# Attention before a soft mixture of experts: block maxima one step earlier, the last batch's slot sums in column halves, A scaled on VectorE, the denominator applied in the relu

## The chip, the cores and the metric

The kernel runs on one core of a Trainium2 chip. The time is device time of one execution in microseconds. The engines of the core are TensorE (PE in the profile, its weight loads PEld), VectorE (DVE), ScalarE (ACT), GpSimd (POOL) and SyncE (SP), which here issues nearly all DMA transfers.

## What is computed

Three layers follow one another, all in float32. The first is a local and block-summary attention over 4 batches, 8 heads, 768 positions and 64 columns per head. A query sees the 31 keys around it, and 24 summaries: the maximum over each block of 32 keys, with the mean of the block's values.

```python
k_sum = k.reshape(B, H, nb, block, D).max(axis=3)
v_sum = v.reshape(B, H, nb, block, D).mean(axis=3)
scores_l = scale * np.matmul(q, k.transpose(0, 1, 3, 2))
scores_s = scale * np.einsum('bhsd,bhnd->bhsn', q, k_sum) + np.log(block)
a = softmax(np.concatenate([np.where(mask_l, scores_l, -1e9), scores_s], axis=-1))
x = np.matmul(a, np.concatenate([v, v_sum], axis=2))     # 3072 tokens x 512
```

The second layer is a soft mixture of 8 experts with 4 slots each. Its slots are sums over all tokens, so nothing of its experts can start before the last token of the attention is through:

```python
logits = x @ phi                                          # 3072 x 32
d = exp(logits - logits.max(0)); d /= d.sum(0) + 1e-9     # over the tokens
slot_input = d.T @ x                                      # 32 x 512
slot_out[e] = np.maximum(slot_input[e] @ w1[e], 0) @ w2[e]
x = softmax(logits, axis=1) @ slot_out
```

The third layer routes each token to the nearest of 8 expert embeddings and applies that expert with a gate.

## The kernel before

**The attention loop.** The unit is a pair of heads (16 pairs: 4 per batch), and each pair has two steps `u` of 384 positions. The even step is u = 2m, the odd one 2m + 1. The loop `for u in range(NU + 11)` with NU = 32 writes out the order of the work by hand: each engine runs its instructions in the order in which the loop emits them. Step u emits the scores `s_pe(u)` (TensorE, tile `s`), the masked maxima `s_max(u)` (VectorE, L316), the subtraction `s_sub(u)` (GpSimd, L329), then for the step two before the product with the values `v_pe(u - 2)` (TensorE, tile `po`, a single PSUM bank) and its division `v_norm` (VectorE, tile `X`), then block sums of the values (`vs`, `vs2`, spread by GpSimd at L267 in even steps), transposes `x_pe` and logits `x_log` of earlier pairs, then the transposes `p_pe(u - 1)` of the probabilities (tile `pt`, copied to `pts` by ScalarE) and at the end the exponentials `s_exp(u)` (ScalarE).

The scores of a pair read keys and block maxima from one tile `kT`. The maxima are made by `t_sum(n)` on VectorE in four instructions (L276, L277, L284, L285): two reductions over 16 keys into `hm`, and two that combine halves into the places in `kT`. In the kernel before, the odd step 2m + 1 ends with `t_sum(m + 1)`, and the next step begins with the scores that read it.

**The slot sums.** `moe_a(b)` takes the running maximum of a batch's logits (`nm_run`, L420) and the exponentials, `moe_b` transposes, `moe_c` multiplies with `X` (TensorE, tile `pa`, L481) and its `moe_c_ev` rescales `A_run` by `al` and adds (L495). `moe_d` makes the combine weights `ce_all` (L507 to L518) in three consecutive steps. For the last batch (b = 3) this is written out at step U_END = 37: `A_run` is scaled by a matmul with the diagonal `dal` (L474), the slots' maxima and denominators go through `si_max`, `si_bc` and `si_den`, the denominator enters the weights `wsl`, and `siT_done` makes `siT` by four matmuls (tile `psi`, L569). Single `keep_warm` matmuls (L589) stand between. The experts' first product `ph` (L756) reads `siT`.

**The loads.** SyncE issues all loads in order: for pair m + 3 at the odd step 2m + 1 its `kT` (484 KB, three buffers), `qT` (384 KB), and two `vw` (390 KB each), and weight tiles of 1024 KB by the list W_STEPS, one every second step up to step 24. A load waits at the head of the queue until its buffer is free. The 32 weight tiles lie in buffers that the attention leaves: `big2` holds `kT`, `qT` and the masked scores, the tile number W_X takes the buffer of an `X`. The first sixteen feed `ph`, the others the product `pO` (L832).

Of the kernel before, what the change touches and what calls it, by code (L numbers as in the profile page):

```python
# [134 lines left out]
def tile_kernel(ctx, tc, qT, kTd, vwd, phi, w1, w2, emb, tau, u1, u2, consts, consts2, out):  # L135
# [11 lines left out]
    siT = cp.tile([P, 4, NSLOT], F32, name="siT")  # L147
    c0r = cp.tile([P, 1], BF16, name="c0r")
# [55 lines left out]
    with ExitStack() as es:  # L204
# [222 lines left out]
        def moe_a2(b):  # L427
            nm, prev = nm_run[:, b : b + 1], nm_run[:, b - 1 : b]
            if b:
# [11 lines left out]
                if b == B - 1:  # L441
                    dal = p3.tile([96, 96], F32, name="dal", bufs=1)
                    nc.vector.tensor_scalar_mul(dal, ident[:96, :96], al)
                    st_["dal"] = dal
# [11 lines left out]
        def moe_b_ev(b):  # L456
            L = sp.tile([P, 2, 2, 96], F32, tag="L", name=f"L{b}")
            pn = st_.pop(("pn", b))
            if b < B - 1:
                nc.vector.tensor_copy(L, pn)  # L460
            else:
                nc.vector.tensor_copy(L[:, 1], pn[:, 1])
                nc.scalar.copy(L[:, 0], pn[:, 0])
            st_["L", b] = L

        def moe_c(b, part=None):

            last = b == B - 1
            if part in (None, 0):
                st_["pa", b] = ps_tr.tile([P, 512], F32, tag="tr", name=f"pa{b}")[0:96, :]  # L470
            pa = st_["pa", b]
            if part == 0:
                for g in range(3):
                    nc.tensor.matmul(  # L474
                        pa[32 * g : 32 * g + 32, :], st_["dal"][:, 32 * g : 32 * g + 32], A_run, start=True, stop=False
                    )
                return
            L, X = st_["L", b], st_["X", b]
            for j in range(2) if part is None else (part - 1,):
                for g in range(3):  # L480
# [4 lines left out]
                        start=j == 0 and not last,  # L485
# [3 lines left out]
        def moe_c_ev(b):  # L489
            pa = st_.pop(("pa", b))  # L490
            if b == B - 1:
                nc.vector.tensor_copy(A_run[:, 0:256], pa[:, 0:256])
                nc.scalar.copy(A_run[:, 256:512], pa[:, 256:512])
            elif b:
# [27 lines left out]
        def si_max():  # L522

            pm = ps_s.tile([P, 512], F32, tag="s", name="pm")
            st_["pm"] = pm
            nc.tensor.transpose(pm[0:1, 0:96], nm_run[:, B - 1 : B], ident[:96, :96])

        def si_max_ev():
            gm = sp.tile([1, NSLOT], F32, tag="gm", name="gm")
            gm3 = sp.tile([1, 3, NSLOT], F32, tag="gm3", name="gm3")  # L530
            nc.vector.tensor_reduce(
                gm, st_["pm"][0:1, 0:96].rearrange("p (g s) -> p s g", g=3), axis=AX.X, op=ALU.min
            )
            nc.vector.tensor_copy(gm3, gm.unsqueeze(1).to_broadcast([1, 3, NSLOT]))
            st_["gm3"] = gm3

        def si_bc():
            nc.tensor.matmul(
                st_["pm"][:96, 96:97], st_["gm3"].rearrange("p g s -> p (g s)"), ones[0:1, 0:1],
                start=True, stop=True,  # L540
            )

        def si_bc_ev():
            gmc = sp.tile([96, 1], F32, tag="gmc", name="gmc")
            fw = sp.tile([96, 2], F32, tag="fw", name="fw")
            nc.vector.tensor_copy(gmc, st_["pm"][:96, 96:97])
            nc.scalar.activation(fw[:, 0:1], nm_run[:, B - 1 : B], AF.Exp, bias=gmc, scale=-1.0)
            nc.vector.tensor_tensor(out=fw[:, 1:2], in0=fw[:, 0:1], in1=sm_run[:, B - 1 : B], op=ALU.mult)
            st_["fw"] = fw

        def si_den():
            pd = ps_s.tile([P, 512], F32, tag="s", name="pd")
            nc.tensor.matmul(pd[:96, 0:1], con[:96, C_SEL : C_SEL + 96], st_["fw"][:, 1:2], start=True, stop=True)
            st_["pd"] = pd

        def si_den_ev():
            rd = sp.tile([96, 1], F32, tag="rd", name="rd")
            wsl = sp.tile([96, NSLOT], F32, tag="wsl", name="wsl")
            nc.vector.tensor_scalar_add(rd, st_["pd"][:96, 0:1], 1e-9)
            nc.vector.reciprocal(rd, rd)  # L560
            nc.vector.tensor_tensor(out=rd, in0=rd, in1=st_["fw"][:, 0:1], op=ALU.mult)
            nc.vector.tensor_scalar_mul(wsl, con[:96, C_SEL : C_SEL + NSLOT], rd)
            st_["wsl"] = wsl

        def siT_done():

            psi = ps_s.tile([P, 512], F32, tag="s", name="psi")
            for c in range(4):
                nc.tensor.matmul(  # L569
                    psi[:, c * NSLOT : (c + 1) * NSLOT], A_run[:, c * P : (c + 1) * P], st_["wsl"],  # L570
                    start=True, stop=True,
                )
            nc.vector.tensor_copy(siT.rearrange("p c s -> p (c s)"), psi[:, 0 : 4 * NSLOT])

        def warm_up():
# [3 lines left out]
            for _ in range(5):  # L579
# [33 lines left out]
        for u in range(NU + 11):  # L613
# [7 lines left out]
            if inr(u - 2):  # L621
# [3 lines left out]
                v_norm(u - 2)  # L625
            if u == 1:
# [13 lines left out]
            if (n := at(u, 4, 2, NPAIR)) is not None:  # L640
                x_pe(n, 1)
                x_ev(n, 1)
# [748 lines left out]
```

## Time and profile before

| | |
|---|---|
| Median of three runs | 275.32 us (273.88 to 280.05) |
| The profiled execution | 275.28 us, of which the profile's span is 273.4 us |
| TensorE busy | 237.8 us, 87% of the span |
| VectorE busy | 152.0 us, 56% |
| ScalarE busy | 127.1 us, 46% |
| GpSimd busy | 90.9 us, 33% |
| Moved by DMA | 72.53 MB, mean 265 GB/s |

The span runs from the first to the last instruction of the program. An engine is counted as busy while one of its instructions runs; waiting is not counted. The attention fills the first 150 us or so, then come the slot sums, the experts of the second layer (to about 202 us), and the third layer. The chain of waits follows the work that ended last back to the start: at each step to what released it. "Idle before" is the time in which an engine had nothing to do, with the instruction that ended it.

### The profile page before, as it was taken

The page shows a single profiled execution, that of the slowest core. Times are in us where ns is not written, and L with a number is a line of the kernel's source. Part 1 is how long each engine was busy: PE and PEld are TensorE (multiplying, and loading weights), DVE is VectorE, ACT ScalarE, POOL GpSimd, SP SyncE. Part 2 cuts the span into 40 slices and gives each one's busy share as a digit, 9 for nine tenths or more (in the row PEclk, how much of TensorE's full clock was granted, in tenths as well). Part 3 has the DMA queues.
Part 4 walks back from the last instruction along what each step waited for, and adds up shares of the span by engine and source line. Part 5 has one row for each costly group of instructions (what it writes and reads, how often), then busy time and mean ns, then how long its engine had stood idle before and what let it go on. Part 6 is the DMA issues. An engine that isn't in the chain of part 4 may idle for free.

```text
span 273.4 us, 7963 instructions
## 1 busy us (share of the span) xinstructions
PE 237.8 (87%) x3070; PEld 156.3 (57%) x3070; DVE 152.0 (56%) x698; ACT 127.1 (46%) x290; POOL 90.9 (33%) x131
## 2 busy tenths in 40 slices
PE   4798988998898878988898899999899998869980
PEld 1477676776766666667675443333375662637760
DVE  2567766767667677587764531133211676645840
ACT  1366456555546556355644311142323677733650
POOL 0456546654475536545642000000101560010000
PEclk9999999999999999999999999999999979977997
DMA  6999989999869997774399999999397000002993
GB/s 212 400 399 386 386 308 331 333 332 334 299 242 339 314 343 256 295 255 136 96 339 316 363 382 380 387 386 380 102 330 283 1 0 1 2 29 95 340 382 113
DMA packets 33658, 72.53 MB, mean 265 GB/s; under 512 B 2712, under 2 KB 4504, under 8 KB 33616
## 3 DMA queue, kind: packets, MB, share of 16 engines
q1 hardware_dynamic: 33552, 71.77, 73.8%
q8 instruction: 26, 0.43, 0.7%
q0 software_dynamic: 64, 0.20, 0.2%
q14 instruction: 16, 0.13, 0.2%
HBM read 65.67 MB, written 6.29 MB: 263 GB/s over the span
## 4 chain that ended last, share of the span: by engine, by line
PE 62%; DVE 23%; DMA 4%; issue 3%; ACT 3%; POOL 1%; SPq 1%; DVEq 0%; ACTq 0%
PE s L301 10%; DVE fix L316 7%; PE po L356 5%; PE ph L756 5%; PE pt L343 5%; PE pO L832 5%; DVE hm L277 4%; PE pht L1049 4%; PE lp L407 3%; DVE X L373 3%; DMA w2e<-in_moe_w_dram 3%; PE pa L481 3%; PE py L1292 2%; PE pd L261 2%; PE py L1294 2%
## 5 line engine op out<-in xcount | busy, mean ns | idle before, releaser
L329 POOL TENSOR_TENSOR fix<-fix,nb 128x360 f32<-128x360 f32 x64 | 49.2, 789 | 62.5 <-DVE nb L316 62.4
L316 DVE CUSTOM_DVE_ANT_0 fix<-s,con 128x120 f32<-128x120 f32 x192 | 41.7, 279 | 35.5 <-PE s L301 35.5
L344 ACT COPY pts<-pt 120x384 f32<-120x384 f32 x64 | 27.6, 482 | 15.1 <-PE pt L343 15.0
L335 ACT ACTIVATE fix<-fix 128x360 f32<-128x360 f32 x64 | 29.2, 510 | 8.3 <-POOL fix L329 8.3
L356 PE MATMUL po<-vw,pts 120*64 120x65 f32 x768 | 29.9, 226 | 1.4 <-POOL vw L267 0.5
L356 PEld LDWEIGHTS po<-vw,pts 120*64 120x64 f32 x768 | 25.3, 137 | 6.9 <-ACT pts L344 3.1
L343 PE MATMUL pt<-con,fix 128*120 128x128 f32 x192 | 27.1, 276 | 0.7 <-ACT fix L335 0.7
L267 POOL COPY vw<-vw 24x780 f32<-24x780 f32 x31 | 25.8, 833 | 3.4 <-issue 1.5
L301 PE MATMUL s<-fix,fix 64*64 64x120 f32 x480 | 19.0, 272 | 8.3 <-DVE fix L284 7.9
L343 PEld LDWEIGHTS pt<-con,fix 128*120 128x120 f32 x192 | 21.1, 138 | 7.3 <-issue 6.2
L301 PEld LDWEIGHTS s<-fix,fix 64*64 64x64 f32 x480 | 14.0, 132 | 12.7 <-DVE fix L284 10.0
L373 DVE TENSOR_TENSOR X<-po,den 128x384 f32<-128x384 f32 x32 | 17.9, 558 | 1.1
L399 ACT COPY xT<-tx 128x384 f32<-128x384 f32 x32 | 15.3, 480 | 6.5 <-PE tx L389 5.7
L1062 DVE CUSTOM_DVE_ANT_0 hlo<-pht,scr 128x1024 fp32r<-128x1024 f32 x11 | 13.3, 1213 | 8.6 <-PE pht L1049 8.6
L389 PE MATMUL tx<-con,X 128*128 128x128 f32 x96 | 16.7, 283 | 0.7 <-DVE X L373 0.7
L1049 PE MATMUL pht<-cT,gs 128*128 128x512 f32 x48 | 16.0, 457 | 0.7 <-ACT hhi L1073 0.5
L1073 ACT ACTIVATE hhi<-pht,scr 128x1024 fp32r<-128x1024 f32 x13 | 14.5, 1116 | 3.7 <-PE pht L1049 3.5
L257 ACT COPY vw<-pd 128x130 f32<-128x130 f32 x16 | 4.3, 268 | 25.6 <-PE pd L261 25.6
L301 PE MATMUL s<-fix 64*64 64x120 f32 x288 | 11.4, 272 | 5.5 <-DVE fix L284 4.8
L316 DVE DVE_READ_ACCUMULATOR2_ANT nb<- 128x1 f32 x192 | 16.0, 83 | 0.2
L832 PE MATMUL pO<-w,hx 128*32 128x512 f32 (+1 forms) x152 | 15.4, 509 | 0.0
L277 DVE TENSOR_REDUCE hm<-fix 128x48 f32<-128x768 f32 x16 | 15.1, 945 | 0.4 <-DMA fix<-in_kT_dram 0.4
(233 smaller groups left out, 371.8 us busy)
## 6 DMA issues: line engine op xcount, KB each, us to landing
w<-in_moe_w_dram SPq DMA_DIRECT2D x30, 1024.0 KB, 9.4
vw<-in_vw_dram SPq DMA_DIRECT2D x32, 390.0 KB, 6.9
fix<-in_kT_dram SPq DMA_DIRECT2D x15, 484.0 KB, 5.3
out_dram<-Y SPq DMA_DIRECT2D x24, 256.0 KB, 2.7
fix<-in_qT_dram SPq DMA_DIRECT2D x15, 384.0 KB, 5.8
w1e<-in_moe_w_dram SPq DMA_DIRECT2D x4, 512.0 KB, 4.5
w2e<-in_moe_w_dram SPq DMA_DIRECT2D x4, 512.0 KB, 9.1
wx<-in_moe_w_dram SPq DMA_DIRECT2D x1, 1024.0 KB, 8.3
```

What stands on the lines that cost most here:

```text
L267: (nc.scalar.copy if n == 0 and par else nc.gpsimd.tensor_copy)(st_["vw", n][row0 : row0 + NB, par].rearrange("p (s x) -> p s x", s=6), vo ...
L277: nc.vector.tensor_reduce(hm[:, 1:49].rearrange("p (c b) -> p c b", b=8), kT[:, 32 + NB :].rearrange("p (c x) -> p c x", x=152)[:, :, 0:12 ...
L301: nc.tensor.matmul(sp[j][64 * i : 64 * i + 64, c, :], qns[n % 3][64 * j : 64 * j + 64, 64 * t : 64 * t + 64], kTs[n % 3][64 * j : 64 * j + ...
L316: nc.vector.tensor_tensor_reduce(out=sms[u % 2][:, j, c, :], in0=sp[:, c, :], in1=con[:, m0 : m0 + KW], scale=-0.125, scalar=3.0e38, op0=A ...
L329: nc.gpsimd.tensor_tensor(out=sm, in0=sm, in1=st_["nb", u][:, j].unsqueeze(2).to_broadcast([P, 3, KW]), op=ALU.subtract)
L335: nc.scalar.activation(sm, sm, AF.Exp, scale=-1.0)
L343: nc.tensor.transpose(pt[:, c, :], sms[u % 2][:, j, c, :], ident)
L344: nc.scalar.copy(pts[:, j], pt)
L356: nc.tensor.matmul(po[64 * i : 64 * i + 64, c, j, :], pts[:, j, c, 64 * i : 64 * i + 64], vw[:KW, i, x0 : x0 + 65], start=True, stop=True,)
L373: nc.vector.tensor_tensor(out=X[:, 3 * h : 3 * h + 3, 2 * hp * D : (2 * hp + 2) * D].rearrange("p c (j d) -> p c j d", j=2), in0=po[:, :, ...
L832: nc.tensor.matmul(po[c][32 * g : 32 * g + 32, 0 : cs.stop - cs.start], hTs[r][:, fc, 32 * g : 32 * g + 32], w[:, g, cs], start=(r, fc) in ...
L1049: nc.tensor.matmul(ph[:, c * 512 : c * 512 + 512], G[:, k * P : (k + 1) * P], cTt(1024 * j + 512 * c, 512), start=True, stop=True,)
```

## The change

It does five things. `t_sum(m + 1)` is emitted at the end of the even step 2m, no longer at the end of the odd step 2m + 1. In the last batch's slot sums `A_run` is scaled and added to on VectorE, as in the other batches, and not by a matmul with `dal`; the sums are made in two column halves with a `psi` of their own. The denominator no longer enters `wsl`: its reciprocal goes into `rdm`, which replaces the constant scale of the relu. `moe_c` of the third batch is split over steps 33 and 34, `moe_d` comes two steps later for every batch, the last `p_pe` comes ahead of the other work of step 32, and the loop is two steps longer. The warm-up has two matmuls, before five, and three weight tiles change their buffers or steps.

```diff
-W_X, W_BIG2, W_BIG3 = 17, (13, 14, 16, 18), (20, 21)
+W_X, W_BIG2, W_BIG3 = 19, (13, 14, 16, 17), (20, 21)
-W_STEPS = (*range(4, 26, 2), 27, 29, 30, 30, 31, 32, 32, 33, 33)
+W_STEPS = (*range(4, 26, 2), 27, 29, 30, 30, 31, 32, 33, 33, 34)
...
+        def moe_last(b):
...
+            nc.vector.tensor_reduce(nm, lp, axis=AX.X, op=ALU.max, negate=True)
+            nc.vector.tensor_tensor(out=nm, in0=nm, in1=prev, op=ALU.min)
+            keep_warm(4)
+            pm = ps_s.tile([P, 512], F32, tag="s", name="pm")
+            nc.tensor.transpose(pm[0:1, 0:96], nm, ident[:96, :96])
+            nc.scalar.activation(LT[:, 1, :], lp, AF.Exp, bias=nm, scale=1.0, accum_out=smb)
+            nc.scalar.activation(al, prev, AF.Exp, bias=nm, scale=-1.0)
+            nc.vector.tensor_reduce(gm, pm[0:1, 0:96].rearrange("p (g s) -> p s g", g=3), axis=AX.X, op=ALU.min)
+            keep_warm(1)
...
+            for j in range(2):
+                nc.tensor.transpose(pn[1][:, 96 * j : 96 * j + 96], LT[:, 1, j * P : j * P + P], ident[:96, :96])
+            nc.scalar.copy(L[:, 1].rearrange("p j x -> p (j x)"), pn[1])
+            pg = ps_s.tile([P, 512], F32, tag="s", name="pg")
+            for g in range(3):
+                nc.tensor.matmul(pg[32 * g : 32 * g + 32, 0:1], gm, ones[0:1, 0:1], start=True, stop=True)
+            keep_warm(1)
+            nc.vector.tensor_copy(gmc, pg[:96, 0:1])
+            nc.scalar.activation(fw[:, 0:1], nm, AF.Exp, bias=gmc, scale=-1.0)
+            nc.vector.scalar_tensor_tensor(
+                out=smb, in0=sm_run[:, b - 1 : b], scalar=al, in1=smb, op0=ALU.mult, op1=ALU.add
+            )
+            nc.vector.tensor_copy(LT[:, 0, :], lp)
+            nc.vector.tensor_tensor(out=fw[:, 1:2], in0=fw[:, 0:1], in1=smb, op=ALU.mult)
+            nc.vector.tensor_scalar_mul(wsl, sel[:, 0:NSLOT], fw[:, 0:1])
+            psi = []
+            for i in range(2):
+                pa = ps_s.tile([P, 512], F32, tag="s", name=f"pl{i}")[0:96, 0:256]
+                for j in range(2):
+                    for g in range(3):
+                        nc.tensor.matmul(
+                            pa[32 * g : 32 * g + 32, :],
+                            L[:, 1, j, 32 * g : 32 * g + 32],
+                            X[:, 2 * g + j, half[i]],
+                            start=j == 0,
+                            stop=j == 1,
+                        )
+                nc.vector.scalar_tensor_tensor(
+                    out=A_run[:, half[i]], in0=A_run[:, half[i]], scalar=al, in1=pa, op0=ALU.mult, op1=ALU.add
+                )
+                if i == 0:
...
+                    nc.tensor.matmul(pd[:, 0:1], sel, fw[:, 1:2], start=True, stop=True)
+                    for j in range(2):
+                        nc.tensor.transpose(
+                            pn[0][:, 96 * j : 96 * j + 96], LT[:, 0, j * P : j * P + P], ident[:96, :96]
+                        )
+                    nc.scalar.copy(L[:, 0].rearrange("p j x -> p (j x)"), pn[0])
+            for i in range(2):
+                psi.append(ps_s.tile([P, 512], F32, tag="s", name=f"psi{i}"))
+                for c in range(2):
+                    x0 = (2 * i + c) * P
+                    nc.tensor.matmul(
+                        psi[i][:, c * NSLOT : (c + 1) * NSLOT], A_run[:, x0 : x0 + P], wsl, start=True, stop=True
+                    )
+                (nc.scalar.copy, nc.vector.tensor_copy)[i](
+                    siT[:, 2 * i : 2 * i + 2].rearrange("p c s -> p (c s)"), psi[i][:, 0 : 2 * NSLOT]
+                )
+            rd = sp.tile([P, 1], F32, tag="rd", name="rd")
+            nc.vector.tensor_scalar_add(rd, pd[:, 0:1], 1e-9)
             nc.vector.reciprocal(rd, rd)
+            nc.vector.tensor_scalar_mul(rdm, con[:, C_RND : C_RND + 2], rd)
...
-            for _ in range(5):
+            for _ in range(2):
...
-        for u in range(NU + 11):
+        for u in range(NU + 13):
...
+            if u == NU:
+                p_pe(u - 1)
+            if u == NU + 1:
+                moe_c(B - 2, 0)
...
+            if u == NU + 2:
+                moe_c(B - 2, 1)
+                moe_c_ev(B - 2)
...
-            if (b := at(u, 16, 8, B - 1)) is not None:
+            if (b := at(u, 16, 8, B - 2)) is not None:
                 moe_c(b)
                 moe_c_ev(b)
             for i in range(3):
-                if (b := at(u, 16 + i, 8, B)) is not None:
+                if (b := at(u, 18 + i, 8, B)) is not None:
                     moe_d(b, i)
-            if inr(u - 1) and u > 1:
+            if inr(u - 1) and 1 < u < NU:
                 p_pe(u - 1)
...
-            if odd and m + 1 < NPAIR:
+            if not odd and m + 1 < NPAIR:
                 t_sum(m + 1)
             if u == U_END:
...
+                moe_last(last)
...
-        nc.scalar.activation(h1s[q], ph, AF.Relu, scale=con[:, C_RND + q // 2 : C_RND + q // 2 + 1])
+        nc.scalar.activation(h1s[q], ph, AF.Relu, scale=rdm[:, q // 2 : q // 2 + 1])
```

## Rows read from the trace of the kernel before

**Rows 1.** Chain of waits, 38 to 48.5 us (start us, us, what).

```profile
42.57 0.84 PE s L301 x24
...
45.15 0.56 DVE X L373
...
45.78 0.87 DVE hm L277
...
46.92 1.05 PE s L301 x24
```

**Rows 2.** Waits: engine line waited for: us in total, times, longest us.

```profile
PE s L301 <- DVE fix L284: 12.7, 14, 1.6
...
PEld po L356 <- ACT pts L344: 3.1, 17, 0.5
```

**Rows 3.** Windows, one pair: stretch, us, busy us of PE, PEld, DVE, ACT, POOL, ...

```profile
38.55:42.50 3.95, 3.95 (x65) 2.95 (x65) 2.30 (x16) 1.55 (x5) 1.85 (x3) 1.00 0.93 346
42.50:46.92 4.42, 3.63 (x83) 2.96 (x82) 3.31 (x19) 2.96 (x8) 2.89 (x4) 1.00 0.97 343
```

**Rows 4.** Timeline of that pair (start us, us, engine, line; idle before in brackets).

```profile
41.39 0.56 DVE L373 TENSOR_TENSOR X<-po,den 128x384 f32<-128x384 f32 x1
...
42.19 1.72 POOL L267 COPY vw<-vw 24x780 f32<-24x780 f32 x2
...
43.51 0.28 DVE L316 CUSTOM_DVE_ANT_0 fix<-s,con 128x120 f32<-128x120 f32 x1 [1.56 <-PE s L301]
```

**Rows 5.** L285 over the kernel (ns min/median/max); timeline rows of step 3.

```profile
L285 DVE TENSOR_TENSOR fix<-hm x16: 300/302/948, 5.1 to 137.1; 128x144 f32<-128x144 f32 x16
...
20.83 1.72 POOL L267 COPY vw<-vw 24x780 f32<-24x780 f32 x2
...
21.76 0.95 DVE L285 TENSOR_TENSOR fix<-hm 128x144 f32<-128x144 f32 x1
```

**Rows 6.** Windows; the last two columns are DMA share and GB/s.

```profile
10.00:20.00 10.00, 8.39 (x183) 6.37 (x181) 6.45 (x45) 6.33 (x15) 5.46 (x9) 1.00 1.03 402
20.00:60.00 40.00, 36.34 (x693) 28.34 (x684) 27.33 (x157) 22.84 (x59) 23.95 (x32) 1.00 0.98 347
```

**Rows 7.** Line L229, issue to landing: all fifteen `kT` loads; the first alone.

```profile
DMA to landing us min/median/max: 3.4/5.3/9.2
...
DMA to landing us min/median/max: 6.6/6.6/6.6
```

**Rows 8.** Timeline of the start, of the attention's end, and of the last `pO`.

```profile
3.47 4.14 PE L580 MATMUL warm<-fix 128*16 128x256 f32 x10 [3.47 <-DMA fix<-in_kT_dram]
...
148.65 0.74 DVE L495 SCALAR_TENSOR_TENSOR A_run<-A_run,al,pa 96x512 f32<-96x512 f32 x1 [1.79 <-PE pa L481]
...
152.76 0.19 DVE L517 RECIPROCAL cs<-cs 128x6 f32<-128x6 f32 x1
...
153.69 1.13 PE L589 MATMUL warm<-con 128*128 128x256 f32 x4
153.81 0.42 DVE L420 TENSOR_REDUCE nm_run<-lp 96x1 f32<-96x256 f32 x1 [0.86 <-PE lp L407]
...
155.32 0.28 ACT L431 ACTIVATE al<-nm_run 96x1 f32<-96x1 f32 x1
...
157.96 1.06 PE L481 MATMUL pa<-X,L 128*32 128x512 f32 x6
...
160.80 1.08 PE L569 MATMUL psi<-wsl,A_run 96*128 96x32 f32 x8
...
162.45 5.36 PE L756 MATMUL ph<-w,siT 128*32 128x512 f32 x48
...
201.01 1.07 PE L832 MATMUL pO<-w,hx 128*32 128x256 f32 x16
```

**Rows 9.** Line L175 from 180 to 186 us: the last weight loads, issue to landing.

```profile
L175 SPq DMA_DIRECT2D w<-in_moe_w_dram x3: 2519/2535/2565, 178.4 to 183.6; - x3
...
DMA to landing us min/median/max: 11.9/13.0/14.2
```

More of the change, by code (lines that the diff above doesn't have):

```diff
@@ L147, in tile_kernel @@
     siT = cp.tile([P, 4, NSLOT], F32, name="siT")
+    rdm = cp.tile([P, 2], F32, name="rdm")
     c0r = cp.tile([P, 1], BF16, name="c0r")
@@ L457, in moe_b_ev @@
             L = sp.tile([P, 2, 2, 96], F32, tag="L", name=f"L{b}")
[L458 to L463, printed above, removed]
+            nc.vector.tensor_copy(L, st_.pop(("pn", b)))
             st_["L", b] = L
         def moe_c(b, part=None):
-            last = b == B - 1
             if part in (None, 0):
                 st_["pa", b] = ps_tr.tile([P, 512], F32, tag="tr", name=f"pa{b}")[0:96, :]
[L471 to L479, printed above, removed]
+            pa, L, X = st_["pa", b], st_["L", b], st_["X", b]
+            for j in range(2) if part is None else (part,):
                 for g in range(3):
@@ L484, in moe_c @@
                         X[:, 2 * g + j, :],
-                        start=j == 0 and not last,
+                        start=j == 0,
                         stop=j == 1,
@@ L490, in moe_c_ev @@
             pa = st_.pop(("pa", b))
[L491 to L494, printed above, removed]
+            if b:
                 nc.vector.scalar_tensor_tensor(
@@ L537, in si_bc @@
[L537 to L543, printed above, removed]
+        def moe_last(b):
+            lp = st_.pop(("lp", b))
+            X = st_["X", b]
+            LT = p2.tile([96, 2, 256], F32, tag="LT", name=f"LT{b}", bufs=1)
+            nm, prev = nm_run[:, b : b + 1], nm_run[:, b - 1 : b]
+            smb = sm_run[:, b : b + 1]
+            al = sp.tile([96, 1], F32, tag="al", name=f"al{b}")
+            L = sp.tile([P, 2, 2, 96], F32, tag="L", name=f"L{b}")
+            gm = sp.tile([1, NSLOT], F32, tag="gm", name="gm")
@@ L556, in si_den_ev @@
-        def si_den_ev():
-            rd = sp.tile([96, 1], F32, tag="rd", name="rd")
-            wsl = sp.tile([96, NSLOT], F32, tag="wsl", name="wsl")
-            nc.vector.tensor_scalar_add(rd, st_["pd"][:96, 0:1], 1e-9)
-            nc.vector.reciprocal(rd, rd)
[L561 to L573, printed above, removed]
+            wsl = sp.tile([96, NSLOT], F32, tag="wsl", name="wsl")
@@ new lines, in moe_last @@
+            sel = con[:96, C_SEL : C_SEL + P]
+            half = [slice(256 * i, 256 * i + 256) for i in range(2)]
+            nc.vector.tensor_reduce(nm, lp, axis=AX.X, op=ALU.max, negate=True)
[4 more added lines that the diff above has]
+            nc.scalar.activation(LT[:, 1, :], lp, AF.Exp, bias=nm, scale=1.0, accum_out=smb)
@@ new lines, in moe_last @@
+            nc.scalar.activation(al, prev, AF.Exp, bias=nm, scale=-1.0)
+            nc.vector.tensor_reduce(gm, pm[0:1, 0:96].rearrange("p (g s) -> p s g", g=3), axis=AX.X, op=ALU.min)
+            keep_warm(1)
+            pn = [ps_tr.tile([P, 512], F32, tag="tr", name=f"pn{b}_{w}")[:, 0:192] for w in range(2)]
+            for j in range(2):
+                nc.tensor.transpose(pn[1][:, 96 * j : 96 * j + 96], LT[:, 1, j * P : j * P + P], ident[:96, :96])
+            nc.scalar.copy(L[:, 1].rearrange("p j x -> p (j x)"), pn[1])
```

47 lines of the change are left out of this document (4 added, 43 removed).

## Prediction

> **What bounds the kernel now.** I read the page's first parts, the chain of waits, the list of waits, and then the timeline of one pair of heads, of the start and of the end of the attention. In the page TensorE is by far the busiest engine, so the question is where it stands still. The chain of waits answers it for the attention, which fills the first 150 us: the chain runs over TensorE from the scores of an even step to those of the odd step, passes to VectorE, runs through the block maxima `hm`, and comes back to the scores of the next even step [rows 1]. One pair of heads is one turn of that loop. In the list of waits the scores stand 14 times behind the maxima (L284), for 12.7 us of TensorE's time [rows 2]. Two windows over one pair show the rest: a turn takes 3.95 + 4.42 = 8.37 us; in the even step TensorE is never idle, in the odd step it is idle for 4.42 - 3.63 = 0.79 us, and that is where `t_sum` is late [rows 3]. Moreover the even scores take 1.05 us, the odd ones 0.84 us [rows 1], since the even ones creep behind the last part of `t_sum`.
>
> **The attention loop.** `t_sum` for the next pair moves from the odd step's end to the even step's end, one step ahead of its use. It issues the same four VectorE instructions and no DMA. What goes is the wait: 12.7 us, and the stretched scores, 14 x 0.20 = 2.8 us; together 15.5 us. A pair would then take TensorE's own work, 3.95 + 3.63 - 0.20 = 7.38 us [rows 3].
>
> What is late next? On VectorE `t_sum` now stands behind the even step's `X` and ahead of the odd step's score maxima, which wait in order behind it. In the pair from 38.55 us the odd maxima start at 43.51, with 1.56 us of idle time before them, after an `X` that ends at 41.95 [rows 4]; `t_sum` takes about 1.4 us (on the chain from the end of the odd step's `X`, 45.71, to the scores at 46.92 [rows 1], and to the end of L285 a little more). It just fits. If it overruns, the odd maxima start late; GpSimd's subtraction, the exponentials and `X` of the odd step follow, and the first to notice on TensorE is the next even step's `po`, because its PSUM bank is freed by that `X`. In the pair shown that `X` ends at 45.71 us [rows 1]; TensorE, without its wait, would be through with the odd step at 42.50 + 3.63 = 46.13 [rows 3] and come to that `po` some 0.8 us later, behind the scores. With a handover taken off, VectorE is 1.1 us ahead, so an overrun under 1.1 us costs nothing.
>
> Here a rule speaks against the new place. GpSimd spreads the block sums (`vw`, L267) from 42.19 us to 43.91 us in the pair shown [rows 4], so the new `t_sum` falls on it. Once already the two met: L285 takes 302 ns in the median, but 948 ns in the step where it met L267 and ended 0.16 us after it [rows 5]. That is 0.65 us a pair, inside the 1.1 us. The Trainium skill ("SBUF — State Buffer", Who interferes with whom) says that a VectorE instruction with two SBUF inputs and a GpSimd instruction that reads SBUF exclude each other for a whole instruction; the trace agrees in that one row, and by this rule it would now happen in every pair.
>
> In six steps (the batch steps of `moe_b` and `moe_c`) `t_sum` also stands behind the copy of `L` or the update of `A_run`, which wait for TensorE; there the 1.1 us are used up. I take 0.15 us each, 1.0 us in all (between 0 and 6 x 0.74, the update's own time [rows 8]). Elsewhere the edit of `moe_a` to `moe_d` is the same work two steps later and is costed at nothing, under TensorE's work, except at the end (below). The attention gains 15.5 - 1.0 = 14.5 us (10 to 16.5).
>
> **The loads.** A pair brings 2672 KB (`kT` 484, `qT` 384, `vw` 780, one weight tile 1024), 2.74 MB. At 7.38 us a pair this asks 371 GB/s. From 20 to 60 us the queues moved 347 GB/s at a share of 0.98; but from 10 to 20 us, with a full queue and the attention running, 402 [rows 6]. So 371 is just within reach, and there is lead: `kT` lands 5.3 us after its issue, 9.2 at most [rows 7], and would be read about 2 x 7.38 - 1.4 = 13.4 us after it. I cost the loads at nothing. The Trainium skill ("SBUF — State Buffer", Summary: rules for kernel authors) counts on about 358 GB/s from HBM; by that a pair would take 7.64 us, and with 0.26 us lost in eleven pairs the sum would be 262.6 us. The 402 GB/s of the trace disagree with it.
>
> Behind the attention the weight tiles must follow. The last half tile lands 11.9 us after its issue at 183.6 us, at 195.5, and its product starts at 201.01: 5.5 us of lead [rows 8, 9]. The late tiles are issued when attention buffers come free, so they come earlier with it. The renumbering of `W_X`, `W_BIG2` and `W_STEPS` only follows the order in which these buffers come free. Cost nothing.
>
> **The start.** Three of five warm-up matmuls go (0.6 x 4.14 = 2.5 us [rows 8]), but the time turns into a wait: `t_sum(1)` now stands ahead of the second step's maxima and waits for the first of the `kT` loads of L229, which takes 6.6 us to land [rows 7], until about 10.6 us. With the 1.4 us of `t_sum` behind that, the maxima come some 1.9 us late (an estimate), and GpSimd's spreading of the first `vw`, behind them in its queue, holds the first `po`. The warm-up rows take 0.41 us apiece, the same 256 columns at 153.69 us 0.28 us [rows 8]: the engine starts at the lower of its two levels (1.2 GHz) and may now stay there longer. Between a gain of 2.5 and a loss of 3 us I take a loss of 0.5.
>
> **The end of the attention.** From the last batch's maxima (L420) to the first expert product (L756) takes 162.45 - 153.81 = 8.64 us [rows 8]. In `moe_last`, counted from the maxima: `al` is ready at 155.60 - 153.81 = 1.79, as before. A copy, two transposes, the slot minimum's matmuls and one keep-warm (half of 1.13), some 1.05 us together, bring TensorE to 2.85. The sums follow by halves: twice the 1.06 us of an L481 row, with a denominator and two transposes (0.6, an estimate from the same rows) between, 5.55. The second half's update on VectorE (half of 0.74, plus a handover) ends at 6.0; half of `psi` (0.54) ends at 6.5. The denominator's chain now runs beside it and meets the path only at the relu, 3.4 us later. The gain is 2.1 us. Against it, the third batch's combine weights stand two steps later, directly ahead of L420 on VectorE: from the start of L495 to the end of L517, the last of them, it took 152.95 - 148.65 = 4.3 us, at most 1.4 of them (an estimate: what ScalarE did ahead of them) a queue that is now gone. L495 itself comes at about 151.4 (`po` of the last step is earlier since `p_pe(31)` moves ahead of `pa`), so the maxima start at 154.3 to 155.7, in place of 153.81: 0.5 to 1.9 us late. With 0.5 the end gains 1.6 us (0.2 to 3.4).
>
> **Sum.** 14.5 - 0.5 + 1.6 = 15.6 us. The profiled execution took 275.28 us (span 273.4), beside a median of 275.32, so both lead to the same: 275.3 - 15.6 = 259.7 us.
>
> **Rivals.**
>
> *The transfers are the bound.* For it: the share of 0.98 from 20 to 60 us [rows 6]. If 347 GB/s is all there is beside a dense attention, a pair takes 2.74 / 0.347 = 7.9 us; the eleven pairs with weights lose 0.5 us each, 5.8 in all: 265.5 us. Against it: 402 GB/s at 10 to 20 us. 13 in 100.
>
> *VectorE becomes the bound.* If GpSimd's copy holds not only L285 but makes the two engines wait in turn, over 1.1 us a pair, VectorE's loop decides; at 7.8 us a pair the attention keeps 14 x 0.56 = 7.8 us and the whole is 275.3 - 7.8 + 0.5 - 1.6 = 266.4 us. For it: the row of 948 ns. Against it: one such row only, and it ended with the copy. 11 in 100.
>
> *The wait only changes its name* (TensorE stands at `po` or `pt` for as long as it stood at the scores): then the start and the end remain, 274.2 us. For it: the weight loads of `po` already wait for ScalarE's `pts`, 17 times. Against it: for 0.2 us a time [rows 2]. 5 in 100.
>
> *Slower than before.* `t_sum` waits on VectorE for `kT`, with the maxima of the running step behind it. With a landing time L the pair takes (L + 1.4) / 2 us, so from L = 15.3 us on the loop is slower than today; at 16.5 us, 8.95 us a pair, it ends at 275.3 + 14 x 0.59 - 1.1 = 282.5 us. For it: faster steps fill the queue, and weight tiles already take longer. Against it: 9.2 us is the most that `kT` took. 4 in 100.
>
> **How the numbers follow.** The forecast has 67 in 100, and its own range is 256 to 263.5 (the ends of the start's and of the attention's terms; they won't all fall one way). With the transfers and with VectorE as the bound it is 91: the range for 8 in 10 is 255.5 to 267. A measurement of this kernel tells about 2% (5.5 us) from no change: faster 0.91, same 0.05 (the wait that changes its name), slower 0.04.
>
> **What would show it.** In the new trace: no row of the scores waiting for L284, pairs of 7.4 us, even scores of 0.85 us; L285 near 0.9 us in every pair, and still no idle time on TensorE; 365 to 375 GB/s from 20 to 90 us. The scores of the last step come some 14 us earlier; L420 to L756 takes 6.5 us. It would be wrong if `po` or `pO` rows wait for DMA or for `X`, or if the maxima of odd steps wait for `kT`.

## The result and the profile after

The kernel after takes 261.5 us in the median of four executions (258.91 to 262.17), the kernel before beside it 275.72 (273.88 to 280.05); the ratio is 0.950, 95% interval 0.941 to 0.958. Two later sets, each with its own runs of the kernel before, gave 0.944 (0.939 to 0.949) and 0.937 (0.932 to 0.943). The ratios leave out single executions that took over 1.5% more than the fastest of their kernel, such as the one of 280.05 us, while the medians count all. The forecast of 259.7 us lies between the medians of the three sets, 259.3, 260.1 and 261.5. The profiled execution is the shortest of its set, 258.91 us; its span is 257.1.

The waits of the kernel after, TensorE first (engine line waited for: us in total, times, longest us). The scores waiting for the maxima, 12.7 us in [rows 2], are gone from the list:

```profile
PE warm L588 <- DMA fix<-in_kT_dram: 3.5, 1, 3.5
PE rank L1148 <- DVE flag L1144: 2.1, 2, 1.4
PE po L357 <- POOL vw L268: 1.9, 2, 1.7
PE phm L1269 <- DVE hlo L1272: 1.2, 1, 1.2
...
PE pm L523 <- DVE nm_run L520: 0.8, 1, 0.8
```

Two windows of one pair, the one that answers to [rows 3] (stretch, us, busy us of PE, PEld, DVE, ACT, POOL, then clock, DMA share, GB/s):

```profile
37.74:41.39 3.65, 3.65 (x66) 2.76 (x65) 2.58 (x17) 2.31 (x7) 1.74 (x3) 1.00 0.97 364
41.39:45.04 3.65, 3.65 (x84) 2.96 (x82) 3.03 (x18) 2.32 (x6) 3.11 (x4) 1.00 1.03 402
```

TensorE is never idle; a pair takes 7.30 us, 8.37 before. The timeline of the same pair shows where `t_sum` (L277 to L286) has gone:

```profile
37.74 0.85 PE L302 MATMUL s<-fix,fix 64*64 64x120 f32 x24
...
40.39 0.56 DVE L374 TENSOR_TENSOR X<-po,den 128x384 f32<-128x384 f32 x1
40.86 0.16 DVE L277 TENSOR_REDUCE hm<-fix 128x1 f32<-128x16 f32 x1
...
42.02 0.30 DVE L286 TENSOR_TENSOR fix<-hm 128x144 f32<-128x144 f32 x1
...
42.48 0.28 DVE L317 CUSTOM_DVE_ANT_0 fix<-s,con 128x120 f32<-128x120 f32 x1 [0.16 <-PE s L302]
...
45.04 0.84 PE L302 MATMUL s<-fix,fix 64*64 64x120 f32 x24
```

It lies in the gap behind the even step's `X`, ends 0.16 us before the odd step's first maxima can start, and the even scores take 0.85 us, not 1.05 [rows 1].

All kernels below are compared by stages, from the starts of four rows of TensorE in the profiled execution: the scores of step 4, of step 30 and of step 31, and the first `ph`. All are us.

| kernel | to step 4 | 4 to 30 | 30 to 31 | 31 to `ph` | `ph` to end | span |
|---|---|---|---|---|---|---|
| before | 21.90 | 115.35 | 4.28 | 20.92 | 110.95 | 273.4 |
| after | 23.27 | 100.70 | 4.15 | 19.26 | 109.72 | 257.1 |
| after, second set | 21.71 | 100.30 | 4.18 | 19.26 | 110.75 | 256.2 |
| after, third set | 21.51 | 101.76 | 4.16 | 19.26 | 112.21 | 258.9 |

The last column but one moves by 2.5 us between executions of one kernel, with TensorE's granted clock in that stretch: its mean is 0.96, 0.94 and 0.93 in the three sets, and 0.94 in the kernel before. The first and the third set (columns as above):

```profile
147.40:257.10 109.70, 94.82 (x629) 52.16 (x629) 47.16 (x112) 44.95 (x79) 12.73 (x26) 0.96 0.57 214
```

```profile
146.70:258.90 112.20, 97.66 (x629) 53.73 (x629) 46.92 (x112) 44.87 (x79) 12.76 (x26) 0.93 0.56 209
```

### The profile page after: what moved, and what is told of

It is laid out like the page before. It is cut to its first block, busy times and chain, and to the rows that moved or that the text cites. A ratio compares the mean times of both kernels' runs of the same rounds, so it can differ in the third digit from the quotient of the medians.

```text
span 257.1 us, 7971 instructions
## 1 busy us (share of the span) xinstructions
PE 233.4 (91%) x3074; PEld 155.5 (60%) x3074; DVE 152.7 (59%) x696; ACT 127.0 (49%) x291; POOL 91.3 (36%) x131
## 4 chain that ended last, share of the span: by engine, by line
PE 77%; DVE 7%; DMA 6%; SPq 2%; issue 2%; ACT 2%; POOL 1%; DVEq 0%; POOLq 0%
PE po L357 10%; PE s L302 8%; PE pt L344 8%; DMA vw<-in_vw_dram 6%; PE pO L829 6%; PE ph L753 6%; PE tx L390 5%; PE pv L250 4%; DVE hlo L1059 3%; PE lp L408 3%; PE pht L1046 3%; PE py L1289 2%; PE pd L262 2%; PE py L1291 2%; PE py L1290 2%; PE pa L465 2%
## 5 line engine op out<-in xcount | busy, mean ns | idle before, releaser
L317 DVE CUSTOM_DVE_ANT_0 fix<-s,con 128x120 f32<-128x120 f32 x192 | 41.5, 277 | 17.7 <-PE s L302 14.5
L357 PE MATMUL po<-vw,pts 120*64 120x65 f32 x768 | 31.0, 229 | 2.5 <-POOL vw L268 1.9
L357 PEld LDWEIGHTS po<-vw,pts 120*64 120x64 f32 x768 | 26.2, 140 | 8.4 <-ACT pts L345 2.8
L268 POOL COPY vw<-vw 24x780 f32<-24x780 f32 x31 | 26.2, 845 | 1.9
L302 PE MATMUL s<-fix,fix 64*64 64x120 f32 x480 | 17.0, 271 | 0.0
L1070 ACT ACTIVATE hhi<-pht,scr 128x1024 fp32r<-128x1024 f32 x13 | 14.5, 1114 | 3.1 <-PE pht L1046 2.8
L1046 PE MATMUL pht<-cT,gs 128*128 128x512 f32 x48 | 15.0, 427 | 1.1 <-ACT hhi L1070 0.5
L250 PE MATMUL pv<-vw,con 120*32 120x130 f32 x384 | 15.4, 294 | 0.0
L753 PE MATMUL ph<-w,siT 128*32 128x512 f32 x128 | 14.8, 596 | 0.5 <-DVE rd L578 0.5
L302 PEld LDWEIGHTS s<-fix,fix 64*64 64x64 f32 x480 | 12.4, 132 | 3.4 <-issue 2.9
```

The costliest lines, as they stand in the source:

```text
L250: nc.tensor.matmul(pv[32 * g : 32 * g + 32, 0:130], con[:KW, b0 : b0 + 32], vw[:KW, par, x0 : x0 + 130], start=c == 0, stop=c == 2,)
L268: (nc.scalar.copy if n == 0 and par else nc.gpsimd.tensor_copy)(st_["vw", n][row0 : row0 + NB, par].rearrange("p (s x) -> p s x", s=6), vo ...
L302: nc.tensor.matmul(sp[j][64 * i : 64 * i + 64, c, :], qns[n % 3][64 * j : 64 * j + 64, 64 * t : 64 * t + 64], kTs[n % 3][64 * j : 64 * j + ...
L317: nc.vector.tensor_tensor_reduce(out=sms[u % 2][:, j, c, :], in0=sp[:, c, :], in1=con[:, m0 : m0 + KW], scale=-0.125, scalar=3.0e38, op0=A ...
L357: nc.tensor.matmul(po[64 * i : 64 * i + 64, c, j, :], pts[:, j, c, 64 * i : 64 * i + 64], vw[:KW, i, x0 : x0 + 65], start=True, stop=True,)
L753: nc.tensor.matmul(ph[32 * g : 32 * g + 32, :], siT[:, kc, :], w[:, g, :], start=kc == 0, stop=kc == 3)
```

## The experiments

**The maxima back, and the maxima alone.** The two kernels undo or make the one edit:

```diff
 (after, label e1_maxima_back)          (before, label e2_maxima_alone)
-if not odd and m + 1 < NPAIR:          -if odd and m + 1 < NPAIR:
+if odd and m + 1 < NPAIR:              +if not odd and m + 1 < NPAIR:
     t_sum(m + 1)                            t_sum(m + 1)
```

> The kernel after, with one part undone: the block maxima of the next pair stand at the end of the odd step again. Theory (the wait of the scores for the maxima was worth about 14.6 us of the 14 gained): all of it comes back, about 276 us, with some 14 waits of the scores for L285, pairs of 8.3 to 8.4 us. Part of the start's loss of 1.4 us goes too, since the second step's maxima no longer stand behind a load: 274.5 to 276. Rival (the gain came with the reordered slot sums, loads and transposes, and the wait would have been hidden anyway): it stays within 2 us of 261.5.

> The kernel before, with that one part alone: the block maxima at the end of the even step, the slot sums, the warm-up and the weights' buffers as they were. Theory: the attention's 14.6 us without the end's 1.7 us; with five warm-up matmuls in front the start loses 1 to 3 us: 275.7 - 14.6 + 1 to 3 = 262 to 264. Rival (the parts only work together: the batch steps, in which the maxima stand behind the update of A_run, eat the gain unless these are moved too): 266 to 272.

With the maxima back: 272.65 us, 0.990 of before (0.987 to 0.993). With the maxima alone: 261.56 us, 0.950 (0.945 to 0.954). The wait returns in the first, as the list of its waits shows:

```profile
PE s L302 <- DVE fix L285: 12.8, 13, 1.6
```

| kernel | to step 4 | 4 to 30 | 30 to 31 | 31 to `ph` | `ph` to end | span |
|---|---|---|---|---|---|---|
| maxima back | 20.71 | 115.14 | 4.28 | 19.27 | 113.01 | 272.4 |
| maxima alone | 22.40 | 102.17 | 4.07 | 20.93 | 111.23 | 260.8 |

The parts are separate. The attention's time goes with `t_sum` alone (115.35 to 102.17, 115.14 when it is undone), the stretch behind it with the edits at the attention's end (19.27 against 20.93): the slot sums, the earlier last `p_pe` and the reordered `moe_c` and `moe_d`, which were not undone one by one. The rival by which the parts only work together is out. With the maxima back the kernel was almost 2 us below the lower end of what was expected. The shorter warm-up brought 1.2 us at the start (20.71 against 21.90), which the theory had not counted, and the 261.5 us that the expectation started from are the highest of the three medians of the kernel after.

**More bytes.** Half of the weight tile before is loaded once more in eleven steps:

```diff
+        if 0 < i < 12:
+            nc.sync.dma_start(out=wload[i - 1][:, :, 0:256], in_=wsrc[i - 1][:, :, 0:256]...)
+        wsrc.append(src)
         wload.append(t)
```

> The kernel after, with 512 KB more to load in each of eleven steps: half of the weight tile before is loaded a second time into the same place. A pair then brings 3184 KB, 3.26 MB, which at 7.30 us asks for 447 GB/s. If the transfers can give about 405 GB/s beside a dense attention (402 were seen in one stretch of before), a pair takes 8.05 us, ten pairs lose 0.75 us each: about 269 us. If the 344 to 367 GB/s of the kernel after are already all there is, a pair takes 8.9 us and more: 277 us and more. If there is room beyond 447, it stays at 261.5.

258.65 us, 0.940 (0.935 to 0.945): not slower than the kernel after. Its attention from step 4 to step 30 takes 122.40 - 22.04 = 100.36 us. Windows of it (columns as above), and from issue to landing of its `kT` loads, line L233:

```profile
24.00:60.00 36.00, 35.56 (x710) 28.11 (x704) 28.52 (x164) 22.65 (x59) 24.01 (x30) 1.00 1.04 394
60.00:100.00 40.00, 39.97 (x780) 30.52 (x772) 32.98 (x184) 25.48 (x69) 24.68 (x32) 1.00 1.05 404
100.00:124.00 24.00, 23.99 (x464) 17.97 (x458) 20.01 (x109) 13.74 (x37) 15.23 (x20) 1.00 0.93 347
```

```profile
DMA to landing us min/median/max: 5.0/8.0/10.0
```

The queue gives 404 GB/s over 40 us with TensorE busy 39.97 of them, 2.95 MB in a pair of 7.30 us, and the kernel after needs 2.74. The surplus that was asked for piles up and is worked off behind 100 us, where less is asked for (238 GB/s from 100 to 124 us in the kernel after): a `kT` lands after 8.0 us in the median and not 5.8, and after 10.0 at most, still inside the 13.4 us at which it is read. The first expectation (a pair of 8.05 us) had the rate right and forgot this lead.

**The start and the end.** Four kernels of one set: the kernel after again; with the second pair's `t_sum` alone at its old place; with five warm-up matmuls; with the last third of the third batch's `moe_d` behind `moe_last`.

```diff
 (e3_first_late)
-if not odd and m + 1 < NPAIR:
+if (u == 1 or (not odd and m)) and m + 1 < NPAIR:
     t_sum(m + 1)
 (e4_five_warm, in warm_up)
-for _ in range(2):
+for _ in range(5):
 (e5_weights_behind)
-if (b := at(u, 18 + i, 8, B)) is not None:
+if (b := at(u, 18 + i, 8, B)) is not None and (b, i) != (B - 2, 2):
     moe_d(b, i)
...
     moe_last(last)
+    moe_d(B - 2, 2)
```

> The kernel after once more, as the measure for the three runs beside it: 0.950 of the kernel before, 261 to 262 us, with the granted clock at 0.5 from about 15 to 18.6 us if that stretch belongs to the kernel and not to the one execution that was profiled.

> The kernel after, with the maxima of the second pair alone at their old place, the end of step 1; all later ones stay where the change puts them. Theory (the start lost 1.4 us because the second step's score maxima stand on VectorE behind a load that lands at about 13 us): those maxima start near 10.2 us as in the kernel before, the first po near 14.2, and the start gives back 1.0 to 2.5 us: 259 to 260.5. Rival (what costs is the lower clock between 15 and 18.6 us, from the shorter warm-up and not from the wait): the clock falls all the same and the gain is under 0.5 us; the scores of step 2 then wait for the maxima of the second pair, 1 us, and the sum is nothing.

> The kernel after, with five warm-up matmuls ahead of the first scores, as before. Theory (the granted clock falls to 0.5 at 15 us since TensorE stood idle while step 1 waited, so the warm-up has no part in it): no gain; the first scores start 2.3 us later, the wait behind them hides most of that, 0 to +1 us. Rival (the shorter warm-up leaves the engine at the lower level): the first scores take 0.85 us in place of 1.61, no stretch at 0.5, and the kernel is 0.5 to 1.5 us faster.

> The kernel after, with the last third of the third batch's combine weights (a sum, an addition, a reciprocal on VectorE, a product on GpSimd) emitted behind the last batch's slot sums, no longer directly ahead of their first maxima. Theory (these maxima start 2 us after the logits are there because VectorE is busy with the third batch): they start at 139 in place of 140.5 us, and the kernel is 1.0 to 1.6 us faster: 260. Rival (the logits, or the transposes behind the keep-warm matmuls, decide the start of the experts anyway): under 0.4 us.

The medians are 259.3, 259.0, 261.54 and 259.17 us, the ratios 0.944, 0.943, 0.940 and 0.942 with intervals of 0.005 to 0.007 to either side: the whole time tells none of them apart. The stages do:

| kernel | to step 4 | 4 to 30 | 30 to 31 | 31 to `ph` | `ph` to end | span |
|---|---|---|---|---|---|---|
| after again | 21.71 | 100.30 | 4.18 | 19.26 | 110.75 | 256.2 |
| first one late | 21.32 | 102.51 | 4.19 | 19.27 | 110.01 | 257.3 |
| five warm-ups | 21.93 | 102.17 | 4.18 | 19.27 | 112.25 | 259.8 |
| weights behind | 21.82 | 103.01 | 4.19 | 18.36 | 111.02 | 258.4 |

*The start.* In the first execution of the kernel after, the granted clock fell: two windows of it, and the timeline's row of the first `po`:

```profile
14.00:18.00 4.00, 2.50 (x44) 2.30 (x48) 2.11 (x15) 1.06 (x3) 2.91 (x4) 0.64 1.03 408
18.00:20.00 2.00, 2.00 (x42) 1.34 (x34) 1.44 (x5) 1.20 (x4) 0.00 (x0) 0.86 1.04 413
```

```profile
15.50 1.57 PE L357 MATMUL po<-vw,pts 120*64 120x65 f32 x24 [1.66 <-POOL vw L268]
```

In the second set the same `po` waits as long, the clock stays, and step 4 starts at 21.71 us, not 23.27:

```profile
9.50 1.55 PE L344 MATMUL pt<-con,fix 128*120 128x128 f32 x6
...
10.63 0.17 DVE L277 TENSOR_REDUCE hm<-fix 128x1 f32<-128x16 f32 x1 [2.07 <-DMA fix<-in_kT_dram]
...
12.02 0.28 DVE L317 CUSTOM_DVE_ANT_0 fix<-s,con 128x120 f32<-128x120 f32 x1
...
14.39 0.83 POOL L268 COPY vw<-vw 24x780 f32<-24x780 f32 x1
...
15.27 0.92 PE L357 MATMUL po<-vw,pts 120*64 120x65 f32 x24 [1.67 <-POOL vw L268]
```

So the fall of the clock belonged to that execution: five more profiles, among them those of the second and the third set, have the same stand of 1.66 us there, and the `po` behind it takes 0.92 us. What belongs to the kernel is the wait: `t_sum(1)` starts at 10.63 us, when its `kT` lands, the second step's maxima at 12.02 in place of 10.18, `po` at 15.27. With the first one late these maxima start at 9.92 us and `po` at 14.57; step 4 starts 0.4 us earlier than in the kernel after, though the first scores came 0.3 us later, with the `qT` load. Five warm-ups shorten the first scores from 1.48 to 0.85 us, and step 4 starts no earlier all the same (21.93 against 21.71), as the wait lies behind.

*The end.* With the weights behind, the last maxima (L519) start 0.13 us behind the logits, in place of 1.92, but only 0.9 us of it arrives at `ph` (1.0 to 1.6 had been expected). Its timeline shows what took over:

```profile
139.44 1.99 PE L597 MATMUL warm<-con 128*128 128x256 f32 x8
139.64 0.41 DVE L519 TENSOR_REDUCE nm_run<-lp 96x1 f32<-96x256 f32 x1
...
140.08 0.23 DVE L520 TENSOR_TENSOR nm_run<-nm_run 96x1 f32<-96x1 f32 x1
140.34 0.36 ACT L493 ACTIVATE ce_all<-ce_all 128x192 f32<-128x192 f32 x1 [2.10 <-POOL ce_all L489]
140.60 0.45 ACT L524 ACTIVATE LT<-lp,nm_run 96x256 f32<-96x256 f32 x1
...
141.28 0.25 PE L523 MATMUL pm<-con,nm_run 96*1 96x96 f32 x1
```

The minimum is ready at 140.3 us, but ScalarE first makes the third batch's exponential (L493), and TensorE is in its four keep-warm matmuls until 141.4. Which of the two holds the path was not run apart; the next kernels take both away.

**Behind, and shorter.** Four kernels of one more set, and the last of them once more in a set of its own:

```diff
 (e8_behind_and_short; e9_with_first_late has the edit of e3_first_late as well)
-if (b := at(u, 18 + i, 8, B)) is not None:
+if (b := at(u, 18 + i, 8, B)) is not None and (b, i) not in ((B - 2, 1), (B - 2, 2)):
     moe_d(b, i)
...
     moe_last(last)
+    moe_d(B - 2, 1)
+    moe_d(B - 2, 2)
 (these two, and e10_short_alone and e11_short_once_more with this alone)
-keep_warm(4)
+keep_warm(1)
```

> The kernel after for a third time, as the measure for the three runs beside it: 259 to 261.5 us, 19.26 us from the last step's scores to the first expert product.

> The kernel after, with the last two thirds of the third batch's combine weights (the exponential on ScalarE too) behind the last batch's slot sums, and one keep-warm matmul in place of four ahead of the slots' minimum. Theory (VectorE's queue by the third batch held the last maxima 2 us; with it gone the exponential in ScalarE's queue and then the four keep-warm matmuls on TensorE hold the path for the 0.9 us that the run before it did not gain): maxima right behind the logits, the last exponential 0.7 us later, and 6.0 us from it to the expert product: 17.3 us from the last scores to that product in place of 19.26, 1.9 us faster than the kernel after. Rival (the granted clock falls behind the shorter keep-warm stretch and gives it back): under 0.5 us.

> As the run before it, and the second pair's block maxima at their old place. Theory: both savings add, 0.4 to 1.0 us at the start to 1.9 at the end: 2.3 to 2.9 us faster than the kernel after, 257. Rival (the start's saving is lost in TensorE's stalls without a releaser, which differ by 2 us from one execution to the next): not told from the run before it.

> The kernel after, with one keep-warm matmul in place of four and nothing else. Theory (VectorE's queue decides; the four matmuls end 0.8 us before the minimum arrives): 19.26 us from the last scores to the expert product stay as they are, 0 to 0.1 us faster. Rival (the four matmuls on TensorE decide): 0.9 us or more faster. If the matmuls keep the clock up, it is slower: the sums behind take longer a row.

> The kernel after with one keep-warm matmul in place of four, a second time. In the first execution TensorE stood 2.1 us before the slots' minimum, and behind it the sums ran at a granted clock of 0.5, 9.7 us from the last maxima to the expert product in place of 6.85. If the idle stretch brings the clock down, it does so again, at the same place: about 9.7 us, and the whole 1 to 3 us above the kernel after. If that execution was a single one, the stretch takes 6.85 us, with the clock at 1.0, and the time is that of the kernel after, 260.

| kernel | median | ratio to before | to step 4 | 4 to 30 | 31 to `ph` | span |
|---|---|---|---|---|---|---|
| after, third set | 260.1 | 0.937 (0.932 to 0.943) | 21.51 | 101.76 | 19.26 | 258.9 |
| behind and short | 258.95 | 0.938 (0.933 to 0.943) | 21.93 | 101.79 | 17.40 | 256.3 |
| with first late | 256.2 | 0.928 (0.923 to 0.933) | 21.38 | 100.29 | 17.40 | 254.4 |
| short alone | 261.88 | | 24.02 | 101.49 | 22.09 | 261.8 |
| short once more | 260.68 | | 21.74 | 101.04 | 22.16 | 258.9 |

The end's 1.9 us came in both kernels that have the edit (17.40 in place of 19.26; 17.3 expected). In the whole time it shows only together with the start: five of the six executions of that kernel took 255.6 to 256.4 us, and the shortest of the kernel after in the same set 257.83. It is ahead of both, of the kernel after by about 1%; its interval and that of the kernel after overlap a little. Some of this lead is luck: in the profiles its attention takes 1.5 us less than that of the two others, and 0.4 to 0.7 of this are stalls that it happened to miss (below).

The shorter keep-warm alone was a miss: 0 to 0.1 us faster was expected, and the stretch takes 22.1 us, 2.8 more than in the kernel after. The windows and rows of the first of these two kernels:

```profile
138.00:142.80 4.80, 2.78 (x23) 1.00 (x21) 2.33 (x7) 1.22 (x3) 1.01 (x2) 0.99 1.05 399
142.80:148.50 5.70, 5.62 (x29) 2.89 (x29) 1.58 (x8) 1.36 (x5) 0.01 (x1) 0.50 0.95 369
```

```profile
142.88 0.32 PE L523 MATMUL pm<-con,nm_run 96*1 96x96 f32 x1 [2.10 <-DVE nm_run L520]
...
145.71 1.93 PE L549 MATMUL pl<-X,L 128*32 128x256 f32 x12
```

TensorE stands 2.10 us before the minimum, the granted clock goes to 0.5, and the sums `pl` take 1.93 us for 1.06. The second time the same 2.10 us stand there, the clock is 0.52 in the 4 us behind, and L519 to `ph` takes 9.74 us (9.68 the first time, 6.85 in the kernel after). In the whole time it hardly shows: the medians are 261.88 and 260.68 us, those of the kernel after 259.3 to 261.5 (1 to 3 us more had been expected of the second). As single executions took only 256.73 and 255.5 us, no ratio stands in the table. Their granted clock over the whole span was 0.979 and 0.989, that of the others 0.955 to 0.975; that the clock didn't fall in them is likely, but they were not profiled.

In the kernel with the weights behind and the same single keep-warm matmul, TensorE stands 0.23 us, the clock is 1.00 from 136 to 146 us, and `pl` takes 1.06 us:

```profile
139.26 0.24 PE L523 MATMUL pm<-con,nm_run 96*1 96x96 f32 x1 [0.23 <-DVE nm_run L520]
...
141.02 1.06 PE L549 MATMUL pl<-X,L 128*32 128x256 f32 x12
```

So in these profiles three matmuls whose result nobody reads are worth 2.8 to 2.9 us as long as VectorE is late, and are not needed once it isn't.

## Why the prediction was right, point by point

The mechanism held: the scores' wait for the maxima is gone, and nothing of its size took its place. That the terms came out so near is in part luck: in the attention and at the end two misses each cancel, and at the start the sign differs from one execution to the next.

**The attention: 14.5 forecast, 14.65 measured** (115.35 to 100.70; 15.05 and 13.59 in the other two sets). The mechanism is shown from both sides by the two kernels with `t_sum` alone moved. The term was made of 15.5 for the wait and the stretched scores, less 1.0 for six batch steps. The 1.0 wasn't there (TensorE is busy 39.94 of the 40 us from 60 to 100 and 29.99 of the 30 behind them); in its place stand 0.4 to 1.3 us of stalls (up to 2.4 in the kernels beside it) that no step had foreseen. Taken without them, the attention of the kernel after takes 99.8 to 100.5 us in the three sets, and 115.35 - 15.5 is 99.85. So the wait and the stretched scores were sized right, and the sum was right by two errors that cancel. That the wait only changes its name is out: `po` waits 2.4 us in all, 1.7 of it once at the start and 0.5 for an `X` behind the last scores, as in the kernel before, and `pt` not at all.

**VectorE's place for `t_sum` fits**, by the 0.16 us that the timeline shows. The step that was wrong is the collision with GpSimd: "L285 near 0.9 us in every pair". L286, as it is called after, and the copies of L268, min/median/max in ns:

```profile
L286 DVE TENSOR_TENSOR fix<-hm x16: 295/301/968, 5.2 to 122.3; 128x144 f32<-128x144 f32 x16
```

```profile
L268 POOL COPY vw<-vw x31: 824/826/955, 14.6 to 128.8; 24x780 f32<-24x780 f32 x31
```

Only once does L286 take 968 ns, where the copy had started 0.02 us before it. Four times the copy starts while L286 runs; then the copy takes 948 to 955 ns and L286 stays at 301 to 305. Twice it was the instruction before it, L285 in this kernel, that came second (756 and 757 ns in place of 184), and twice it met a product of GpSimd (324 ns). So whichever comes second waits, except that seven VectorE instructions which start in the last 0.11 us of a copy are not held. The prediction had charged VectorE in every pair and not asked who comes first. The Trainium skill ("SBUF — State Buffer", Who interferes with whom) says that issue order decides who blocks; the trace agrees in these nine meetings. The price for VectorE was 0.6 to 0.7 us in three pairs of sixteen and 0.1 in two, and never on TensorE's path; VectorE is not the bound.

**The loads cost nothing**: 352 GB/s from 20 to 90 us (365 to 375 said) and 367 from 24 to 60, `kT` 8.9 us after its issue at most, no `pO` row that waits for DMA, and no maxima behind the start that wait for a `kT` (the rival that ended slower). The rival that the transfers are the bound had 13 in 100; the kernel with more bytes shows that it was far off. The 358 GB/s that the Trainium skill ("SBUF — State Buffer", Summary: rules for kernel authors) counts on are less than what moved here: 404 GB/s over 40 us of that kernel.

**The start: a loss of 0.5 forecast, 1.37 lost in the first profile, and 0.2 to 0.4 gained in the two other sets.** The term joins two that the runs separate. The shorter warm-up is worth 1.2 us where `t_sum` stands at its old place (20.71 with the maxima back, one profile). The wait of `t_sum(1)` costs 0.8 to 1.0 against that kernel (21.51 and 21.71), but 0.2 to 0.4 against the one with the first one late (21.32), so its price is known to half a us only. Its mechanism is the one that was forecast: maxima 1.84 us late (1.9 said), GpSimd's spreading behind them, `po` behind that. That the engine stays longer at its lower level came true as well, and the wait hides it: with two warm-ups the first scores take 1.48 to 1.68 us, not 0.85, and in the second set the `pt` at 9.50 us still takes 1.55 us, where six such rows take 0.87 later. What cost 1.6 us in the first profile is something else, the fall of the clock behind the stand before `po`, which the prediction didn't have.

**The end: 1.6 forecast, 1.66 measured in all three sets.** L519 to `ph` takes 6.85 us (6.5 said, 8.64 before), and the maxima come 0.13 us later, counted from the last scores (12.41 against 12.28), where 0.5 to 1.9 was said and 0.5 taken. These two misses, 0.35 and 0.37 us, cancel. The first is a term left out: the working ended with `psi`, whose rows end 6.4 us behind the start of L519 (6.5 said), and `ph` reads `siT`, which ScalarE and VectorE copy from it first. The rows of VectorE's half:

```profile
145.62 1.29 PE L571 MATMUL psi<-wsl,A_run 96*128 96x32 f32 x8
...
146.95 0.23 DVE L574 COPY siT<-psi 128x64 f32<-128x64 f32 x1 [0.72 <-PE psi L571]
```

The logits themselves are there 1.7 us sooner than before (10.5 us behind the start of the last scores, not 12.2). That VectorE's queue by the third batch holds them was right, and the kernels with the weights behind show its price: 1.9 us once the two waits that stand behind it are taken away too.

**Sum**: 14.65 - 1.37 + 1.66 = 14.94, with 0.13 between steps 30 and 31 and 1.23 behind `ph`: the 16.3 us between the two spans. The 1.23 can't be credited to the change: in the other two sets that stretch takes 110.75 and 112.21, with the clock.

## What to carry to other kernels

Where an engine waits for a small piece of preparation once per turn, move the preparation one turn ahead into a gap of its own engine, and check three things in one turn of the timeline: the gap's length, who comes next in that queue, and when the data it reads has landed. The first turn needs its own look, as its data may not be there yet. A wait that is taken off a path shows the next ones that stood behind it, and its full worth comes only when these are gone too: here one edit gave 0.9 us alone, another lost 2.8 alone, and together with a third, not run alone, they made 1.9.

## What the runs showed of the hardware that was not expected

**TensorE's stalls with no releaser sit at fixed places in its instruction stream, multiples of 256 instructions apart.** Once TensorE runs without a wait, rows with idle time "issue" appear, a different amount in each execution. One stall of the kernel after, the same of the kernel with five warm-ups, and two of the kernel with the first one late:

```profile
53.76 0.42 PE L302 MATMUL s<-fix 64*64 64x120 f32 x3 [0.43 <-issue]
```

```profile
52.12 0.46 PE L302 MATMUL s<-fix 64*64 64x120 f32 x9 [0.34 <-issue]
```

```profile
53.06 0.42 PE L302 MATMUL s<-fix 64*64 64x120 f32 x3 [1.19 <-issue]
...
66.74 0.65 PE L250 MATMUL pv<-vw,con 120*32 120x130 f32 x15 [0.58 <-issue]
```

With six more matmul rows in front, the stall comes six rows earlier in the same tile (nine are left, not three): 844 matmul rows of the trace come before it in each. Of all of TensorE's instructions, weight loads and waits included, 1729 come before it. The twelve profiles with the maxima early hold 29 such stalls of 0.15 us or more in their attentions, and all have, to within one, 705, 1473, 1729, 2241, 2497, 3265, 3521 or 4033 instructions before them: numbers that are multiples of 256 apart. The page lists a DMA queue of kind "instruction" with 26 packets, 0.43 MB; in the trace each has 16384 bytes, 64 for each of 256 instructions, and the kernel after has 6284 TensorE instructions, 24.5 times 256. Windows of 0.25 us of the kernel with the first one late hold its packets at 50.75 and at 64.50 us (queue, kind: packets, MB, share):

```profile
q8 instruction: 1, 0.02, 23.3%
...
q8 instruction: 1, 0.02, 24.4%
```

Each of the 29 stalls ends 2.2 to 2.6 us behind the start of such a packet. In the second set of the kernel after the packet starts 3.0 us before the instruction with 1729 before it, and there is no stall. This fits code of TensorE that is loaded in pieces of 256 instructions (about 125 matmuls with their weight loads), and comes just in time when TensorE never waits. The counts speak for it; no run here has changed the code to test it, nor why a piece comes late. The kernel before and the one with the maxima back show no such row in their attentions; that their waits for the maxima cover them is likely, and not shown.

**The clock can fall behind a short stand, and doesn't always.** Behind the 2.10 us before `pm` it was at 0.50 and 0.52 in both profiles; behind the 1.66 us before the first `po` it fell in one profile of six; behind the 0.79 us before `pm` in none of seven. In the first kernel with the shorter keep-warm alone the rows at the start stay at the lower level to about 20 us: the first `po` takes 1.57 us in place of 0.92, and step 4 starts at 24.02, though the clock is recorded as 1.00 there: the rows, and not the record alone, tell the level.
